# A spectral layer and a gated convolution: three `a1` buffers, another opening, another order on VectorE

## Chip, cores, metric

One Trainium2 chip, the program on one of its cores. The metric is the device time of that core in microseconds; the time of a run is its whole device time, and the span of a profile runs from the core's first to its last instruction.

## What is computed

For 8 sequences of 3136 rows and 256 columns:

```python
X = rfft(x, axis=1)                         # 1569 frequencies
Yr = Xr @ w_r - Xi @ w_i + b_r
Yi = Xr @ w_i + Xi @ w_r + b_i
Y  = soft-threshold(Yr, 0.01), soft-threshold(Yi, 0.01)
y  = irfft(Y, n=3136, axis=1)
h  = relu(y @ w_in)                         # 256 -> 1024
c  = 3-tap convolution of h along the rows, per column
out = (h * sigmoid(c)) @ w_out              # 1024 -> 256
```

`moe_w_in`, `moe_conv_w` and `moe_w_out` arrive as 64-bit floats, so the kernel makes 32-bit values out of their bits itself ("conversion" below).

## The kernel before

The Fourier transform of length 3136 = 49 x 64 is done as two stages of matrix products with a scratch array in HBM between them, and the inverse transform likewise.

*First phase (lines 122 to 479).* Stage 1 (`stage1`) multiplies a tile of `x` (`xr`, 98 partitions, 4 columns `j`, 256) with the matrix `f1`, in two halves of one matmul each; ScalarE copies each half from PSUM to a tile `a1`, and after the second half a DMA stores `a1` to the scratch array `sc1[b]` (392 KB). A batch has 8 such tiles, 16 halves. For batch 0 all of it is done ahead of the loop by `stage1_head`, which has tiles of its own (`ha`) for all eight, and copies by ScalarE and VectorE in turn. For the other batches 112 halves are spread over the loop; `halves()` yields one at a time, and asks for the next tile of `x` when one is used up (three buffers). The list `due` in the loop says how many halves must have been given by the end of each step: 2, 5, 9, 13, 16 for steps 0 to 4, then 3 a step, from step 11 on 2.6 a step on average, until 112 are given in step 40.

The loop has steps `it` of 0 to 52. Three stages of work on 50 items (`batch`, group of four residues) stand one step apart:

- `stage2(it)`: for t in 0, 1 eight transforms with the table `t2` (loaded in slices of four groups), from the tile `a2` that was read back from `sc1`. ScalarE copies the imaginary part to `d` and casts both parts to `fh`; VectorE makes `d` the difference (L306) and `fl` the remainder of `fh` (L307), since products are made from two rounded parts. Then ScalarE casts `d` into `fh` (L309), and VectorE makes "`fl` from `d`" (L311). There is one `d`.
- `mix(it - 1)`: 36 matmuls with the weights, in three PSUM tiles `ps_mx` of one buffer each, in the order c = 2, 0, 1. After c = 2 VectorE adds the bias (L333, `p1`), after c = 0 and 1 it makes `v` (L337, twice each).
- `threshold(it - 2)`: ScalarE's `r` (L346), VectorE's L347 on `v`, ScalarE's cast `sh` (L349), GpSimd's `sl` (L350), which has one buffer.
- `stage3(it - 3)`: 12 matmuls from `sh` and `sl`, ScalarE's copy `z1`, a store to `sc2`.

The order on TensorE, and in the loop also that on VectorE and ScalarE, is the order in which the Python code issues instructions (`manual_schedule`). So the generators are advanced by hand: `some(two, 1)` runs `stage2` to its next `yield`, `some(mx, 8)` issues the next eight matmuls of the mix, `one(k)` a half of stage 1 if the step still has more than `k` to give, `back(n)` up to `n` turns of the conversion. The other queues, SyncE's with the DMAs among them, and all engines ahead of the loop are ordered by a planner with its own costs; `issue_after(ins)` puts what a block issues on `ins`'s queue behind `ins`.

The conversion (`later`) has three turns a step. A turn ends at each `yield`; a `yield "act"` closes the step for it, and at the step's end one more turn issues an operation on ScalarE. It starts in step `WP0` = 7, and the turns run out in step 47.

*Second phase (lines 482 to 603).* For each batch `stage4` reads `sc2` and makes the two parts `yh`, `yl` of the spectral output; `up` multiplies with `w_in`, ScalarE and VectorE do the convolution and the gate, `down` multiplies with `w_out`. The first `up` needs all eight pieces of `stage4` of batch 0.

The body of a loop step before, which the change reorders:

```python
some(two, 1)
th = threshold(...)
ss[it - 2] = next(th, None)      # r and L347
back(2)
some(two, 1)
some(mx, 8); one(1)
some(th, 1)                      # sh and sl
some(two, 1); some(mx, 5)        # L309; p1
...
back(1)
some(two, 1)                     # L311
```

Of the kernel before, what the change touches and what calls it, by code (L numbers as in the profile page):

```python
# [9 lines left out]
F32 = mybir.dt.float32  # L10
# [8 lines left out]
B, S, D, FF = 8, 3136, 256, 1024  # L19
# [9 lines left out]
JC = 4  # L29
# [72 lines left out]
def spectral_ffn_kernel(ctx: ExitStack, tc: tile.TileContext, x, w_r, w_i, b_r, b_i,  # L102
                        w_in, conv_w, w_out, fwd1, fwd2, inv1, inv2, out):
    nc = tc.nc
    K1, K2, KQ, KI = 2 * R, 2 * SP, 2 * R2, 4 * (U + 1)
# [16 lines left out]
    with ExitStack() as ab:  # L122
        stg = ab.enter_context(tc.tile_pool(name="stg", bufs=1))
        wbp = ab.enter_context(tc.tile_pool(name="wbp", bufs=2))
        s1p = ab.enter_context(tc.tile_pool(name="s1p", bufs=2))
# [18 lines left out]
        def split(dst_hi, dst_lo, src):  # L144
            nc.scalar.copy(dst_hi, src)
            nc.vector.tensor_tensor(dst_lo, src, dst_hi.bitcast(F32), op=ALU.subtract)
# [4 lines left out]
        def load_t2(g):  # L151
            sl = slice(g * UG, min((g + 1) * UG, U + 1))
            return nc.sync.dma_start(t2[:, sl, :], fwd2v[:, sl, :])

        def load_mix():

            raw = [stg.tile([P, NT, D], F32, name=f"wm_raw{k}", tag="raw", bufs=2) for k in range(2)]
            for k in range(2):
                ld = nc.sync.dma_start(raw[k], (w_r, w_i)[k].rearrange("(t p) e -> p t e", p=P))
            split(wmix_hi[:, :, 0, :], wmix_lo[:, :, 0, :], raw[1])  # L160
            for k, op in ((1, ALU.subtract), (2, ALU.add)):
                w = stg.tile([P, NT, D], F32, name="wm", tag="wm")
                nc.vector.tensor_tensor(w, raw[0], raw[1], op=op)
                split(wmix_hi[:, :, k, :], wmix_lo[:, :, k, :], w)
            return ld
# [85 lines left out]

        def stage1(b, jc, xr):

            a1 = s1p.tile([K1, JC, D], F32, name="a1", bufs=2)
            for j in range(0, JC, 2):
                ps = ps1.tile([K1, 2, D], F32, name="ps_s1")
                nc.tensor.matmul(ps, f1, xr[:, j:j + 2, :], start=True, stop=True)  # L257
                nc.scalar.copy(a1[:, j:j + 2, :], ps)
                if j + 2 == JC:
                    nc.sync.dma_start(sc1[b][:, jc * JC:(jc + 1) * JC, :], a1)  # L260
                yield None

        def stage1_head(xs, b=0):

            with tc.tile_pool(name="ha", bufs=1, reuse_waits="tile") as ha:
                for jc, xr in enumerate(xs):
                    a1 = ha.tile([K1, JC, D], F32, name=f"ha{jc}")
                    for j in range(0, JC, 2):
                        k = (jc * 2 + j // 2) % 4
                        if k < 3:  # L270
                            ps = psm.tile([K1, 2, D], F32, name="ps_s1h", tag=f"ps_mx{k}")
                        else:
                            ps = ps1.tile([K1, 2, D], F32, name="ps_s1")
                        nc.tensor.matmul(ps, f1, xr[:, j:j + 2, :], start=True, stop=True)  # L274
                        if j:
                            nc.vector.tensor_copy(a1[:, j:j + 2, :], ps)
                        else:
                            nc.scalar.copy(a1[:, j:j + 2, :], ps)
                    st = nc.sync.dma_start(sc1[b][:, jc * JC:(jc + 1) * JC, :], a1)
            return st  # L280

        def load_a2(b, g):
            a2 = a2p.tile([KQ, UG, D], F32, name="a2")
            if g < NG:
                rows = slice(g * 4 * UG, (g + 1) * 4 * UG)
                ld = nc.sync.dma_start(a2, sc1[b][rows].rearrange("(u q) j d -> (q j) u d", q=4))
            else:
                for k in range(UG):
                    ld = nc.sync.dma_start(a2[0:R2, k, :], sc1[b + k][4 * U:K1].rearrange("q j d -> (q j) d"))
            return a2, ld  # L290
# [51 lines left out]
        def threshold(v):  # L342
            sh = wk.tile([K2, UG, D], F32R, name="sh")
            sl = wk.tile([K2, UG, D], F32R, name="sl", bufs=1)
            r = wk.tile([K2, UG, D], F32, name="r", bufs=1)
            nc.scalar.activation(r, v, AF.Relu, bias=mlam)  # L346
            nc.vector.scalar_tensor_tensor(v, v, LAM, r, op0=ALU.add, op1=ALU.min)  # L347
            yield sh, sl
            nc.scalar.copy(sh, v)  # L349
            SL_ENG.tensor_tensor(sl, v, sh.bitcast(F32), op=ALU.subtract)  # L350
            yield None
# [17 lines left out]
        def some(g, n):  # L369
            for _ in range(n):  # L370
                next(g, None)
# [5 lines left out]
        items = [(b, g) for b in range(B) for g in range(NG)]  # L377
        for b in (0, UG):
            items.insert(items.index((b + UG - 1, 0)), (b, NG))
        n_it = len(items)  # L380
        firsts = [(b, jc) for b in range(B) for jc in range(NQ)]
        WP0 = NG + 1
        a2s = {}
        load_f1()
        with tc.tile_pool(name="hx", bufs=1, reuse_waits="tile") as hx:
            xh = []
            for p in range(NQ):
                xr, ld = load_x(hx, 0, p, parts=2 if p == 0 else 1, tag=f"hx{p}")
                xh.append(xr)
            with tc.issue_after(ld.ins):  # L390
                st = stage1_head(xh)
        asked = []

        def ask():
            asked.append(load_x(s1p, *firsts[NQ + len(asked)], bufs=XRB)[0])

        def halves():
            for n in range(NQ, len(firsts)):
                yield from stage1(*firsts[n], asked[n - NQ])
                while len(asked) < n - NQ + XRB and len(asked) < len(firsts) - NQ:  # L400
                    ask()

        first = halves()
        with tc.issue_after(st.ins):
            ld = load_mix()
        with tc.issue_after(ld.ins):
            ld = load_t2(0)
        ab.enter_context(tc.manual_schedule(engines={mybir.EngineType.PE}))
        with tc.issue_after(ld.ins):
            ask()  # L410
            some(first, 2)
            a2s[0], ld = load_a2(*items[0])
        with tc.issue_after(ld.ins):
            load_bias()
            a2s[1], ld = load_a2(*items[1])
            for _ in range(2):
                ask()
        ab.enter_context(tc.issue_after(ld.ins))
        wkf, wk, cab, io = [ab.enter_context(tc.tile_pool(name=nm, bufs=n, reuse_waits="tile"))
                            for nm, n in (("wkf", 2), ("wk", 2), ("cab", 1), ("io", 2))]  # L420
# [3 lines left out]
        i1_hi = cab.tile([K2, U + 2, KQ], F32R, name="i1_hi")  # L424
        i1_lo = cab.tile([K2, U + 2, KQ], F32R, name="i1_lo")
        background = later()
        given, held = 2, []
        xs, vs, ss, i1s = {}, {}, {}, {}
        ab.enter_context(tc.manual_schedule(engines={mybir.EngineType.DVE, mybir.EngineType.Activation}))
        for it in range(n_it + 3):  # L430
            xs[it], vs[it - 1] = [], []
            two = stage2(items[it][1], a2s.pop(it), xs[it]) if it < n_it else iter(())
            mx = mix(xs.pop(it - 1), vs[it - 1]) if 0 <= it - 1 < n_it else iter(())
            due = (2, 5, 9, 13, 16)[it] if it < 5 else 16 + 3 * (it - 4) if it <= 10 else 34 + 13 * (it - 10) // 5
            n_a, given = due - given, due
            work = 3 if WP0 <= it < n_it else 0

            def one(k=0):
                some(first, n_a > k)

            def back(n):
                for _ in range(n if work else 0):
                    if not held:
                        held[:] = [0] * (next(background, None) == "act")

            if it <= NG:
                with tc.issue_after(ld.ins) if it + 2 < NG else ExitStack():
                    if it + 3 <= NG:
                        load_t2(it + 1)
                    if it + 3 == NG:  # L450
                        load_t2(NG - 1)
                        load_t2(NG)
                    i1s[it] = load_inv1(it)
            some(two, 1)
            th = threshold(vs.pop(it - 2)[0]) if 0 <= it - 2 < n_it else iter(())
            ss[it - 2] = next(th, None)
            back(2)
            some(two, 1)
            some(mx, 8)
            one(1)  # L460
            some(th, 1)
            some(two, 1)
            some(mx, 5)
            if it - 1 in i1s:
                split(*i1s.pop(it - 1))
            back(1)
            some(two, 1)
            some(mx, 5 if n_a > 3 else 9)
            one(2)
            some(mx, 9)  # L470
            one(3)
            some(mx, 64)
            if held:
                held[:] = [0] * (next(background, None) == "act")
            if 0 <= it - 3 < n_it:
                stage3(*items[it - 3], ss.pop(it - 3))
            one(0)
            if it + 2 < n_it:
                a2s[it + 2], ld = load_a2(*items[it + 2])
# [148 lines left out]
```

## Time and profile before

| | |
|---|---|
| median of 3 runs (lowest, highest) | 1773.59 us (1771.73, 1774.48) |
| profiled execution | 1775.9 us |
| its span | 1774.1 us |
| mean granted TensorE clock | 0.987 |
| busy: TensorE, its weight loads, VectorE, ScalarE, GpSimd | 1730.7, 1608.3, 1487.7, 1209.1, 118.5 us |
| HBM read, written | 86.02 MB, 77.59 MB |

PE is TensorE's matmuls, PEld its weight loads, DVE VectorE, ACT ScalarE, POOL GpSimd, SP SyncE, on whose queue all DMAs are issued. "L311" is line 311 of the kernel. A row of a timeline has start, duration, engine, line, operation, output<-inputs, shape, count, and in brackets the idle time of the engine before it and who ended it. Neighbouring instructions of one line are merged (x4). One 32-bit matmul counts as two in the rows.

### The profile page before, as it was taken

What the parts mean: (1) busy time and instruction counts of PE and PEld (TensorE: products, weight loads), DVE (VectorE), ACT (ScalarE), POOL (GpSimd) and SP (SyncE); (2) the same over time, 40 slices, a digit from 0 to 9 for tenths busy, and PEclk for the clock granted to TensorE, in tenths of its full rate; (3) what the DMA queues carried; (4) which work ended last, traced back from release to release, by engine and by line L of the source; (5) the groups of instructions that cost most, each with busy time, mean ns of one, the idle gap of its engine ahead of it and who ended that gap; (6) DMA issues with size and microseconds to landing.
All of it is one profiled execution on the core that took longest, in us unless ns stands there. A gap on an engine that the chain in (4) does not pass through costs nothing.

```text
span 1774.1 us, 28820 instructions
## 1 busy us (share of the span) xinstructions
PE 1730.7 (98%) x11872; PEld 1608.3 (91%) x11872; DVE 1487.7 (84%) x1757; ACT 1209.1 (68%) x1565; POOL 118.5 (7%) x54
## 2 busy tenths in 40 slices
PE   6999999999888999999999999999999999999999
PEld 2788888888888999999999999999999999999998
DVE  2778898898994988888888888888888888888887
ACT  2567677677554777777777777777777777777766
POOL 0122222222221000000000000000000000000000
PEclk8999999999988999999999999999999999999999
DMA  8777677666424110111111111111101111100001
GB/s 249 223 236 243 213 230 251 219 224 217 127 93 129 38 40 22 38 46 46 50 48 47 46 40 49 50 40 50 49 21 40 49 50 40 49 22 21 22 21 42
DMA packets 108304, 165.47 MB, mean 93 GB/s; under 512 B 8492, under 2 KB 86316, under 8 KB 108174
## 3 DMA queue, kind: packets, MB, share of 16 engines
q1 hardware_dynamic: 108174, 163.64, 29.1%
q8 instruction: 94, 1.54, 0.3%
q14 instruction: 36, 0.29, 0.0%
HBM read 86.02 MB, written 77.59 MB: 92 GB/s over the span
## 4 chain that ended last, share of the span: by engine, by line
PE 92%; DVE 3%; DMA 3%; issue 1%; ACT 1%; SPq 0%; POOL 0%; ACTq 0%
PE acc L557 31%; PE ps_h L529 31%; PE ps_mx L329 9%; PE ps_s L510 7%; PE ps_s L257 5%; PE ps_s L301 4%; PE ps_s L360 3%; DVE v L337 1%; DMA sc<-a 1%; DMA t<-in_fwd_dram 1%; PE ps_s1h L274 1%; ACT r L346 1%; DMA xr<-in_x_dram 0%; DMA z<-sc 0%; DVE p L333 0%
## 5 line engine op out<-in xcount | busy, mean ns | idle before, releaser
L557 PE MATMUL acc<-wout,gh 128*128 128x256 f32 x3136 | 567.4, 280 | 0.0
L529 PE MATMUL ps_h<-yh,win 128*128 128x450 f32 x1792 | 550.1, 368 | 0.0
L538 DVE SCALAR_TENSOR_TENSOR c<-h,cw,c 128x896 f32<-128x896 f32 x448 | 513.5, 1148 | 38.9 <-ACT c L536 37.3
L557 PEld LDWEIGHTS acc<-wout,gh 128*128 128x128 f32 x3136 | 490.1, 188 | 5.1
L557 PE MATMUL acc<-wout,gl 128*128 128x256 f32 x1568 | 437.4, 280 | 0.0
L531 ACT ACTIVATE h<-ps_h 128x900 f32<-128x900 f32 x224 | 207.4, 926 | 260.4 <-PE ps_h L529 260.4
L529 PEld LDWEIGHTS ps_h<-yh,win 128*128 128x128 f32 x1792 | 339.0, 189 | 26.1 <-DVE yl L517 0.4
L529 PE MATMUL ps_h<-yl,win 128*128 128x450 f32 x896 | 329.4, 368 | 0.0
L544 DVE TENSOR_TENSOR gl<-c,gh 128x896 fp32r<-128x896 f32 x224 | 243.2, 1089 | 76.1 <-ACT gh L543 74.6
L557 PEld LDWEIGHTS acc<-wout,gl 128*128 128x128 f32 x1568 | 293.8, 188 | 0.6
L540 DVE TENSOR_TENSOR c<-h,c 128x896 f32<-128x896 f32 x224 | 243.4, 1087 | 48.1 <-ACT c L539 48.1
L543 ACT CAST gh<-c 128x896 fp32r<-128x896 f32 x224 | 211.1, 943 | 70.3 <-DVE c L540 68.3
L539 ACT ACTIVATE c<-c 128x896 f32<-128x896 f32 x224 | 213.0, 951 | 8.3 <-DVE c L538 4.5
L329 PE MATMUL ps_mx<-wmix_hi,fl 128*128 128x256 f32 x600 | 188.0, 313 | 7.6 <-DVE fl L311 7.6
L329 PE MATMUL ps_mx<-wmix_hi,fh 128*128 128x256 f32 x600 | 185.5, 309 | 1.8 <-DVE p L333 1.5
L529 PEld LDWEIGHTS ps_h<-yl,win 128*128 128x128 f32 x896 | 169.3, 189 | 10.9
L536 ACT ACTIVATE c<-h,cw 128x896 f32<-128x896 f32 x168 | 176.1, 1048 | 2.2 <-DVE gl L544 0.2
L329 PE MATMUL ps_mx<-wmix_lo,fh 128*128 128x256 f32 x600 | 171.1, 285 | 0.0
L350 POOL TENSOR_TENSOR sl<-v,sh 128x1024 fp32r<-128x1024 f32 x50 | 118.3, 2366 | 423.3 <-PE ps_s L360 321.6
L337 DVE TENSOR_TENSOR v<-ps_mx,p 64x512 f32<-64x512 f32 x200 | 137.5, 687 | 7.7 <-PE ps_mx L329 4.8
L329 PEld LDWEIGHTS ps_mx<-wmix_hi,fl 128*128 128x128 f32 x600 | 115.5, 192 | 21.1 <-issue 12.0
L510 PEld LDWEIGHTS ps_s<-i,z 100*128 100x128 f32 x1024 | 130.4, 202 | 4.6 <-DVE yl L517 2.2
(84 smaller groups left out, 1963.6 us busy)
## 6 DMA issues: line engine op xcount, KB each, us to landing
z<-sc SPq DMA_DIRECT2D x64, 400.0 KB
xr<-in_x_dram SPq DMA_DIRECT2D x63, 392.0 KB
a<-sc SPq DMA_DIRECT2D x48, 512.0 KB
sc<-z SPq DMA_DIRECT2D x48, 512.0 KB
out_dram<-o SPq DMA_DIRECT2D x27, 896.0 KB
sc<-a SPq DMA_DIRECT2D x56, 392.0 KB
sc<-ha SPq DMA_DIRECT2D x8, 392.0 KB
win_bits<-in_moe_w_in_dram SPq DMA_DIRECT2D x4, 512.0 KB
```

Source lines behind the costliest of these rows:

```text
L329: nc.tensor.matmul(ps[c][:, k, :], lt, rh, start=(n == 0), stop=(n == len(mm) - 1))
L337: nc.vector.tensor_tensor(v[dst, :, k, :], ps[c][src], p1[src, c], op=ALU.add)
L510: nc.tensor.matmul(ps[:, t, j * K1:(j + 1) * K1], z2[:, j, t * P:(t + 1) * P], i2, start=(j == 0), stop=(j == JG - 1), skip_group_check=True)
L529: nc.tensor.matmul(ps[:, a, 0:CH + 2], lt, rh, start=(n == 0), stop=(n == len(mm) - 1))
L531: nc.scalar.activation(h, ps[:, :, 0:CH + 2], AF.Relu)
L536: nc.scalar.mul(c, h[:, :, 0:CH], cw[:, 0, f:f + 1])
L538: nc.vector.scalar_tensor_tensor(c, h[:, :, k:k + CH], cw[:, k, f:f + 1], c, op0=ALU.mult, op1=ALU.add)
L539: nc.scalar.activation(c, c, AF.Sigmoid)
L540: nc.vector.tensor_tensor(c, h[:, :, 1:CH + 1], c, op=ALU.mult)
L543: nc.scalar.copy(gh, c)
L544: nc.vector.tensor_tensor(gl, c, gh.bitcast(F32), op=ALU.subtract)
L557: nc.tensor.matmul(acc[m // 2][:, m % 2, :], lt[:, sl], rh[:, f, :], start=(f == 0 and n == 0 and m % 2 == 0), stop=(f == NF - 1 and n == ...
```

## The change

- The tile `a1` of stage 1 gets three buffers instead of two.
- The opening. The weights' load and split (`load_mix`) and the first slice of `t2` are issued right behind the loads of `x` for batch 0, ahead of `stage1_head` in the code, instead of behind its last store. Behind that store now comes `a2` of step 0 at once, then the first tile of `x` for the loop, the bias, `a2` of step 1, two more tiles of `x`. The first two halves of stage 1, which were issued ahead of step 0, are given in step 0 (`given` starts at 0), where they come behind its transforms. TensorE's order by hand begins a little later in the code.
- In a loop step both `t` of `stage2` come first. `threshold` is cut in three: `r`; L347; `sh` and `sl`. L347 stands behind `p1`, L311 right behind L347, and `sh` and `sl` behind the mix's c = 0 matmuls have begun. On VectorE: both pairs of L306 and L307, a turn of the conversion, L333, a turn, L347, L311, a turn, L337.
- The conversion starts in step 5, again with three turns a step, one at each of three places.

```diff
-            a1 = s1p.tile([K1, JC, D], F32, name="a1", bufs=2)
+            a1 = s1p.tile([K1, JC, D], F32, name="a1", bufs=3)
...
             nc.scalar.activation(r, v, AF.Relu, bias=mlam)
+            yield sh, sl
             nc.vector.scalar_tensor_tensor(v, v, LAM, r, op0=ALU.add, op1=ALU.min)
-            yield sh, sl
+            yield None
             nc.scalar.copy(sh, v)
...
             with tc.issue_after(ld.ins):
+                load_mix()
+                load_t2(0)
                 st = stage1_head(xh)
...
         with tc.issue_after(st.ins):
-            ld = load_mix()
-        with tc.issue_after(ld.ins):
-            ld = load_t2(0)
-        ab.enter_context(tc.manual_schedule(engines={mybir.EngineType.PE}))
+            a2s[0], ld = load_a2(*items[0])
         with tc.issue_after(ld.ins):
             ask()
-            some(first, 2)
-            a2s[0], ld = load_a2(*items[0])
-        with tc.issue_after(ld.ins):
             load_bias()
             a2s[1], ld = load_a2(*items[1])
             for _ in range(2):
                 ask()
+        ab.enter_context(tc.manual_schedule(engines={mybir.EngineType.PE}))
...
-        given, held = 2, []
+        given, held = 0, []
...
-            work = 3 if WP0 <= it < n_it else 0
+            work = 5 <= it < n_it
...
-            some(two, 1)
+            some(two, 2)
             th = threshold(vs.pop(it - 2)[0]) if 0 <= it - 2 < n_it else iter(())
+            some(mx, 8)
+            back(1)
             ss[it - 2] = next(th, None)
-            back(2)
-            some(two, 1)
-            some(mx, 8)
             one(1)
-            some(th, 1)
             some(two, 1)
             some(mx, 5)
             if it - 1 in i1s:
                 split(*i1s.pop(it - 1))
             back(1)
+            some(th, 1)
             some(two, 1)
+            back(1)
             some(mx, 5 if n_a > 3 else 9)
             one(2)
+            some(th, 1)
             some(mx, 9)
             one(3)
             some(mx, 64)
```

## Prediction

> **What bounds the kernel now.** I read the table of stretches first, cut where the chain of waits changes its character: opening loads, filling, steady first phase, last steps of the first phase, hand-over, second phase. Columns: stretch, length, busy time of PE, PEld, DVE, ACT, POOL with instruction counts, granted clock, DMA share, GB/s.
>
> ```profile
> 0.00:24.00 24.00, 18.69 (x32) 6.42 (x32) 5.59 (x10) 6.17 (x10) 0.20 (x4) 1.00 0.78 242
> 24.00:44.00 20.00, 7.82 (x26) 4.99 (x27) 5.84 (x11) 5.37 (x10) 0.00 (x0) 0.66 0.98 256
> 44.00:101.00 57.00, 51.80 (x327) 41.27 (x325) 41.99 (x65) 34.07 (x58) 8.95 (x4) 0.94 0.70 213
> 101.00:442.00 341.00, 340.55 (x2433) 293.05 (x2434) 301.12 (x493) 242.50 (x391) 82.25 (x36) 1.00 0.72 231
> 442.00:529.00 87.00, 75.72 (x585) 71.75 (x584) 83.64 (x126) 49.23 (x76) 22.39 (x10) 0.96 0.37 117
> 529.00:569.00 40.00, 35.32 (x221) 34.45 (x221) 15.86 (x22) 16.10 (x17) 4.70 (x2) 0.76 0.41 133
> 569.00:1774.00 1205.00, 1200.83 (x8256) 1156.33 (x8255) 1033.63 (x1033) 855.69 (x1005) 0.00 (x0) 1.00 0.13 40
> ```
>
> TensorE is never idle for long in 101 to 442 and in 569 to 1774: 1546 of 1774 us can change only if TensorE's own work does, and the diff leaves every matmul in place. What is open is 0 to 101, bound by loads (DMA 0.98 busy in 24 to 44), and 442 to 569, where VectorE is busy 83.64 of 87 us and then the hand-over to the second phase follows.
>
> The chain of waits through the opening (start, length, what):
>
> ```profile
> 24.10 4.86 DMA sc<-ha
> 32.37 10.85 DMA t<-in_fwd_dram
> ...
> 53.69 8.00 DMA sc<-a
> 62.41 2.02 PE ps_s L257 x2
> 64.44 2.35 PE ps_mx L329 x11
> 66.78 1.71 PE ps_s L257 x2
> ...
> 90.85 6.51 DMA sc<-a
> 97.38 3.94 DMA a<-sc
> ```
>
> Three places: the head's last store lands at 28.96 and only then may step 0's `a2` be asked for; step 1 starts at 43.22, when the second slice of `t2` has landed; at 53.69 ScalarE waits 8 us for the store of an `a1` of which there are two.
>
> How long a step is in the steady part, from the chain's last piece of step 40, a half of stage 1, which ends at 441.38 where step 41 begins:
>
> ```profile
> 440.52 0.86 PE ps_s L257 x2
> ```
>
> Step 6 starts when the load asked for at 97.38 has landed, at 101.4. 35 steps to 441.38 are 9.71 us each. The due list gives 112 - 19 = 93 halves to them, 2.66 a step at 0.86, 2.29 us. So TensorE needs 9.71 - 2.29 = 7.4 us for a step without halves, and from step 41 on there are none.
>
> VectorE's rows of step 41, the first of these, in order:
>
> ```profile
> 443.21 0.42 DVE L306 TENSOR_TENSOR d<-ps_s,d 128x256 f32<-128x256 f32 x1 [1.92 <-ACT fh L305]
> 443.55 0.68 DVE L307 TENSOR_TENSOR fl<-ps_s,fh 128x512 fp32r<-128x512 f32 x1
> 444.26 1.23 DVE L347 SCALAR_TENSOR_TENSOR v<-v,r 128x1024 f32<-128x1024 f32 x1
> 445.40 0.69 DVE L196 SCALAR_TENSOR_TENSOR wout_e<-wout_bits,wout_e 128x512 int32<-128x512 int32 x1
> 446.00 0.42 DVE L197 TENSOR_SCALAR wout_m<-wout_bits 128x512 int32<-128x512 int32 x1
> 446.34 0.42 DVE L306 TENSOR_TENSOR d<-ps_s,d 128x256 f32<-128x256 f32 x1
> 446.67 0.68 DVE L307 TENSOR_TENSOR fl<-ps_s,fh 128x512 fp32r<-128x512 f32 x1
> 447.27 1.29 DVE L333 TENSOR_TENSOR p<-ps_mx,bias 128x512 f32<-128x512 f32 x2
> 448.46 0.69 DVE L311 TENSOR_TENSOR fl<-d,fh 128x512 fp32r<-128x512 f32 x1
> 449.06 2.81 DVE L337 TENSOR_TENSOR v<-ps_mx,p 64x512 f32<-64x512 f32 x4
> ```
>
> From 443.21 to 451.87 is 8.66 us; the two conversion operations take 446.34 - 445.40 = 0.94 of it. 7.7 us is thus VectorE's own step, a little over TensorE's 7.4. The later steps are longer for a reason that three rows show: the group of L311 over 441 to 530 (count, busy, mean ns), step 44's L311, and GpSimd's row beside it.
>
> ```profile
> L311 DVE TENSOR_TENSOR fl<-d,fh 128x512 fp32r<-128x512 f32 x9 | 12.9, 1433 | 0.0
> ```
> ```profile
> 476.38 1.80 DVE L311 TENSOR_TENSOR fl<-d,fh 128x512 fp32r<-128x512 f32 x1
> ```
> ```profile
> 475.27 2.36 POOL L350 TENSOR_TENSOR sl<-v,sh 128x1024 fp32r<-128x1024 f32 x1 [7.33 <-ACT sh L349]
> ```
>
> L311 takes 0.69 in step 41 and 1.80 in step 44, where it starts inside GpSimd's `sl` (475.27 to 477.63) and ends 0.55 after it. VectorE's other rows of step 41 read PSUM for one input; L311 reads `d` and `fh`, both in SBUF. The rule in the Trainium skill, SBUF — State Buffer, section Who interferes with whom, is that such an operation and a GpSimd one that reads SBUF exclude each other for a whole instruction, the first to start winning; the trace agrees, 1.80 against 0.69.
>
> The hand-over: VectorE's last work of step 49, then the chain.
>
> ```profile
> 527.02 2.12 DVE L337 TENSOR_TENSOR v<-ps_mx,p 64x512 f32<-64x512 f32 x3
> ```
> ```profile
> 534.96 2.36 POOL sl L350
> 537.37 1.56 PE ps_s L360 x11
> ...
> 544.45 2.04 PE ps_s L510 x16
> 546.51 5.68 DMA z<-sc
> 552.32 16.61 PE ps_s L510 x80
> ```
>
> **The change part by part.**
>
> *Third `a1`.* Removed: the wait from 53.69 to 61.70. Its price on TensorE: the next 2 + 11 + 2 matmuls take 2.02, 2.35 and 1.71 us (62.41 to 68.49), where halves take 0.86 and 11 of the mix some 1.3 (7.4 less 1.8 for the transforms and 1.4 for stage 3, for 36). That is 3.1 us lost to a slow clock behind the pause, and the pause itself is the one row in the list of waits from 50 to 64 that names it:
>
> ```profile
> PE ps_s L257 <- ACT a L258: 3.8, 1, 3.8
> ```
>
> Together 6.9. Next in line are the loads of `x`: DMA is 0.70 busy over this stretch, so they can come earlier, but not for nothing. Bounds: 0 (a load of `x` is as late) and 6.9; I take 6.5, nearer the upper end because of the 0.30 of free DMA.
>
> *Opening loads.* The weights (2 x 256 KB) and the first `t2` slice go ahead of the head's stores, in a stretch with DMA 0.78 busy; at 242 GB/s they are 3.2 us. But step 0's `a2` still waits for the last store, which they push back by about 1 us (the stores queue behind them and catch up in the 0.22 of free time), and now nothing stands between store and `a2`: DMA rests for the 3.94 us of a lone `a2` load (97.38) less its transfer of 512 KB, 2 us. What was moved past the pause is one `x` tile (392 KB by its shape, 1.6 us), which now follows `a2`. Ahead of `t2`'s second slice, for which step 1 waits, stands the same list as before. So step 1 starts between 3 us earlier (no pause) and 4 later; by the bytes I take 1.5 later. The three weight splits (five VectorE operations of the 0.69 kind, three on ScalarE) fall into the head, where VectorE is busy 5.6 of 24 us: nothing, if the queues hold them behind the copies whose data come first; if not, they hold up copies, PSUM and TensorE (a rival).
>
> *Two halves into step 0*: they leave the place ahead of step 0's transforms and stand between these and step 1, in the wait for `t2`: nothing; without that wait 2 x 0.86.
>
> *Steps 2 to 5* are then TensorE's own. Before step 6 stand the store of the 16th half and the load behind it (6.51 + 3.94 us), with the same distance as now, but DMA has to carry the same bytes in some 5 us less: I give back 0.5. **Opening: +1.5 - 6.5 + 0.5 = -4.5 us.**
>
> *Steady steps*: in a step VectorE now does both `d`/`fl` pairs, `p`, then L347 and L311, then the four L337. ScalarE's `r` runs beside the first; `sh` and GpSimd's `sl` come later, but `sl` had to wait for stage 3 at the end of the step anyway. The first L337 moves back by at most 1.9 us (1.23 + 0.69), and what it frees is needed only by the next step's mix. VectorE is busy 301 of 341 us: cost 0, and if that slack is gone up to 1 us a step (a rival).
>
> *Late steps, 41 to 49.* (a) L311 now follows L347 at once, while `sl` has to wait for `sh`, which has to wait for L347: L311 is through before `sl` starts, and the four L337 (2.81 us, one input in PSUM) cover the 2.36 of `sl`. Gone: 9 x (1.43 - 0.69) = 6.7 us. (b) `r` waits for the last L337 of the step before; L347 stood right behind it and now stands behind 3 us of other work. (c) Conversion has three slots a step as before, starting in step 5 instead of 7. Counting the generator's turns, the last lands in step 45, not 47 (nor 40), and of the 14 VectorE operations now in 41 to 47 ten remain. So nine steps at 7.7 and ten operations at some 0.54 (0.69 and 0.42 overlapping by 0.08): 69.3 + 5.4 = 74.7 us from 443.21, against 529.14 - 443.21 = 85.9 now. **-11.2 us.** Bounds: nothing but the four operations and half of L311's loss, -5.5; and TensorE's 7.4 for all nine steps, -13.9.
>
> *Hand-over.* At the end of step 49 the mix of the last item no longer waits for a blocked L311. Stage 3 of item 48 now ends at 538.9, 9.8 us behind VectorE's 529.14. With the pieces in a row it is the last mix part and stage 3 (1.4 + 1.4), then `sl` behind `sh` (2.4), then 1.4: some 7.5. The last `sl` and its stage 3 follow with the same spacing or less. **-2 us** (0 to -3). The loads behind the stores (5.68) and the 16.61 us I leave.
>
> Sum: -4.5 - 11.2 - 2 = -17.7. The profiled execution took 1775.9 us (span 1774.1 and 1.8 around it), which gives 1758.2; the median of the runs, 1773.6, is 2.3 lower, so 1755.9.
>
> **Rivals.**
>
> *The opening gives nothing (22%).* Either `x` is as late as `a1` was, or weight splits stand in VectorE's queue ahead of copies whose data are there. For it: DMA 0.98 busy right behind the head. Against: 0.70 where the wait is. -13.2 or, with the head held up by 4 us, -9: 1760 to 1764.5.
>
> *The hand-over stays at full clock (13%).* The 16.61 us are 80 matmuls at half clock:
>
> ```profile
> 555.00:560.00 5.00, 5.00 (x26) 5.00 (x25) 1.26 (x2) 2.00 (x2) 0.00 (x0) 0.50 0.34 90
> ```
>
> At the 2.04 us for 16 just before, they would take 10.2, so -6.4 more: 1749.5. It needs a shorter pause ahead of them. The Trainium skill, TensorE: Matmul & The Clock Gate, Part 1, would have the clock return after some 3.4 us of sustained work; the trace does not agree, busy 5.00 of 5.00 at 0.50 for over 16 us. By the rule the stretch would cost about 5 us less already today, and the change would move nothing there.
>
> *Late steps do not fall to 7.7 (10%).* ScalarE or the order on TensorE then sets some 8.6 (what step 41 took): -3 instead of -11.2, 1764.
>
> *No change, or slower (7%).* L337 behind L347 and L311 makes the mix of the next step wait for PSUM in the steady part. At 17.7/35 = 0.5 us a step it cancels the rest (3% for that), beyond it decides (4%); at 1 us a step +35 - 17.7: 1791. Against: VectorE's 40 us of slack there, and the step in which those results are not wanted.
>
> **How the numbers follow.** My case has 48%, 1752 to 1759 by itself. The range is 1747 to 1766: it holds the first three rivals' times and leaves out the last rival, a head held up for longer, and two rivals at once. A measurement of this kernel cannot tell 0.2% (3.5 us) from no change: faster 0.93, the first four cases; same 0.03 and slower 0.04, the last rival's two halves.
>
> **What would show it.** No 8 us wait for an `a1` store in the chain; step 6's transforms near 97; L311 at 0.69 in the late group; last conversion operation in step 45; step 49's last L337 near 513; the 80 matmuls at 16 to 17 us. Wrong if the late group keeps 1.4, if the head ends after 26, or if TensorE shows idle time between 101 and 440.

## The result and the profile after

The changed kernel takes 1758.15 us (median; 1753.32 to 1759.99) against 1773.59 (1771.73 to 1775.54) for the kernel before: ratio 0.9908, 95% interval 0.989 to 0.9926. The forecast was 1755.9, with a range of 1747 to 1766. The sum came out; two of its three terms did not. In the changed kernel L347 to L350 are L348 to L351, stage 3's L360 is L361, `stage4`'s L510 is L509, `up`'s L529 is L528.

The profiled execution of the changed kernel is its slowest, 1759.99 (span 1758.2). The table of stretches, cut at the same places and with the same columns:

```profile
0.00:24.00 24.00, 17.95 (x29) 6.05 (x30) 6.04 (x12) 5.94 (x10) 0.20 (x4) 1.00 0.82 235
24.00:44.00 20.00, 7.51 (x24) 4.33 (x22) 5.22 (x9) 5.00 (x10) 0.00 (x0) 0.72 0.74 209
44.00:101.00 57.00, 51.72 (x339) 42.62 (x340) 40.31 (x66) 34.34 (x59) 9.43 (x4) 0.95 0.78 241
101.00:442.00 341.00, 341.00 (x2425) 293.46 (x2425) 298.16 (x495) 242.05 (x391) 81.61 (x35) 0.99 0.72 229
442.00:529.00 87.00, 81.04 (x671) 78.42 (x671) 81.54 (x133) 55.69 (x83) 26.86 (x12) 1.00 0.39 128
529.00:569.00 40.00, 37.44 (x222) 35.48 (x221) 19.57 (x24) 19.81 (x22) 0.58 (x1) 0.83 0.45 130
```

TensorE is never idle from 101 to 442. The DMA share falls from 0.98 to 0.74 in 24 to 44, where the loads set the pace, and rises by only 0.04 in 0 to 24. In busy time over 0 to 44 that is 24 x 0.82 + 20 x 0.74 = 34.5 us, against 38.3 before: 3.8 us less carried. The chain of waits through the opening shows where these are missed:

```profile
26.63 4.83 DMA sc<-ha
...
35.74 11.19 DMA t<-in_fwd_dram
46.93 0.14 issue
47.06 3.37 PE ps_s L301 x16
...
88.82 7.12 DMA sc<-a
95.95 3.90 DMA a<-sc
99.85 0.14 issue
99.98 2.75 PE ps_s L301 x16
102.74 1.71 PE ps_mx L329 x8
```

Step 1 starts at 47.06, 3.7 us later than before (43.35). The 8 us wait for an `a1` store is gone, and step 6 starts at 99.98 (before 101.45). But the matmuls behind that pause take longer (2.75 and 1.71 us, at a granted clock of 0.62 over both; before 2.02 and 0.94, at 1.00), and step 41 starts at 441.36, before 441.22. In the profiles the opening gave nothing.

The late steps did: VectorE's rows at both ends, the last operation of the conversion, GpSimd's `sl` beside the L337 of step 49, and the group of L311 over 441 to 530.

```profile
443.35 0.42 DVE L306 TENSOR_TENSOR d<-ps_s,d 128x256 f32<-128x256 f32 x1 [1.17 <-ACT fh L305]
```
```profile
481.57 0.68 DVE L210 TENSOR_TENSOR wout<-wout_m,wout_rest 128x512 fp32r<-128x512 f32 x1
```
```profile
514.48 2.81 DVE L337 TENSOR_TENSOR v<-ps_mx,p 64x512 f32<-64x512 f32 x4
515.22 2.41 POOL L351 TENSOR_TENSOR sl<-v,sh 128x1024 fp32r<-128x1024 f32 x1 [5.26 <-ACT sh L350]
```
```profile
L311 DVE TENSOR_TENSOR fl<-d,fh 128x512 fp32r<-128x512 f32 x9 | 6.1, 680 | 0.0
```

From 443.35 to 517.29 are 73.94 us, where 85.93 were; L311 takes 0.68 us instead of 1.43, and is over before `sl` starts; the L337 beside `sl` keep their 0.7 us each. The conversion ends in step 45, at 482.25. The hand-over follows, in the chain:

```profile
521.91 0.39 PE ps_s L361
522.30 3.35 PE ps_s L509 x31
525.65 4.71 DMA z<-sc
530.50 2.00 PE ps_s L509 x16
...
535.73 6.04 DMA z<-sc
541.77 0.14 issue
541.90 10.53 PE ps_s L509 x48
552.43 6.19 PE ps_h L528 x24
```

From the last L337 of step 49 to the first `up` (552.14) are 34.85 us, before 39.50. The second phase takes 1206.06 against 1205.46. So by stretches: opening +0.1, late steps -12.0, hand-over -4.7, second phase +0.6; together -16, which is the difference of the spans (15.9).

### The profile page after: what moved, and what is told of

It reads as the page before. It is cut to its first block, busy times and chain, and to the rows that moved or that the text cites. A ratio compares the mean times of both kernels' runs of the same rounds, so it can differ in the third digit from the quotient of the medians.

```text
span 1758.2 us, 28865 instructions
## 1 busy us (share of the span) xinstructions
PE 1721.6 (98%) x11872; PEld 1602.2 (91%) x11872; DVE 1472.0 (84%) x1757; ACT 1206.8 (69%) x1565; POOL 118.7 (7%) x54
## 4 chain that ended last, share of the span: by engine, by line
PE 93%; DMA 2%; DVE 2%; issue 1%; ACT 0%; SPq 0%; DVEq 0%; ACTq 0%
PE ps_h L528 31%; PE acc L556 31%; PE ps_mx L329 11%; PE ps_s L509 6%; PE ps_s L257 5%; PE ps_s L301 5%; PE ps_s L361 3%; DMA t<-in_fwd_dram 1%; DMA z<-sc 1%; DVE v L337 0%; DMA sc<-a 0%; DVE p L333 0%; DMA sc<-ha 0%; DVE fl L307 0%; DVE v L348 0%
## 5 line engine op out<-in xcount | busy, mean ns | idle before, releaser
L528 PE MATMUL ps_h<-yh,win 128*128 128x450 f32 x1792 | 550.6, 368 | 0.0
L528 PEld LDWEIGHTS ps_h<-yh,win 128*128 128x128 f32 x1792 | 339.4, 189 | 26.1 <-DVE yl L516 0.4
L528 PE MATMUL ps_h<-yl,win 128*128 128x450 f32 x896 | 329.7, 368 | 0.0
L528 PEld LDWEIGHTS ps_h<-yl,win 128*128 128x128 f32 x896 | 169.4, 189 | 11.0
L351 POOL TENSOR_TENSOR sl<-v,sh 128x1024 fp32r<-128x1024 f32 x50 | 118.5, 2370 | 410.7 <-PE ps_s L361 254.1
L337 DVE TENSOR_TENSOR v<-ps_mx,p 64x512 f32<-64x512 f32 x200 | 137.4, 687 | 2.9
L301 PEld LDWEIGHTS ps_s<-t,a 128*128 128x128 f32 (+1 forms) x800 | 99.7, 198 | 39.6 <-issue 28.8
L509 PEld LDWEIGHTS ps_s<-i,z 100*128 100x128 f32 x1024 | 128.1, 198 | 5.8 <-issue 3.0
```

Of the source, the lines that this page charges most:

```text
L301: nc.tensor.matmul(ps[:, k], a2[0:rows, k, t * P:(t + 1) * P], t2[0:rows, u, :], start=(k == 0), stop=(k == UG - 1), skip_group_check=True)
L509: nc.tensor.matmul(ps[:, t, j * K1:(j + 1) * K1], z2[:, j, t * P:(t + 1) * P], i2, start=(j == 0), stop=(j == JG - 1), skip_group_check=True)
L528: nc.tensor.matmul(ps[:, a, 0:CH + 2], lt, rh, start=(n == 0), stop=(n == len(mm) - 1))
```

## Experiments

Marks used below are those of the prediction: start of a step's transforms, "late" from VectorE's first `d` of step 41 to the last L337 of step 49, "hand-over" from there to the first `up`. The kernels were run in three groups of four. Each group has a chip of its own, on which the kernel before was run too (its medians: 1775.5, 1775.0, 1776.4); a ratio is always to the kernel before in the same group.

### Parts of the change

**Old opening**, with three `a1`, the new loop, conversion from step 5.

```diff
-                load_mix()
-                load_t2(0)
                 st = stage1_head(xh)
...
-            a2s[0], ld = load_a2(*items[0])
+            ld = load_mix()
+        with tc.issue_after(ld.ins):
+            ld = load_t2(0)
         with tc.issue_after(ld.ins):
             ask()
+            some(first, 2)
+            a2s[0], ld = load_a2(*items[0])
```

> The changed kernel with the opening of before (weights, first t2 slice and the first two halves back in their old places); three a1 buffers and the new order of the steps stay. In the changed kernel the head's last store is issued at 26.63 instead of 24.10, step 1 starts at 47.06 instead of 43.35 and step 6 at 99.98 instead of 101.45. Theory A, the new opening costs: the weight splits hold up the head and DMA rests behind its last store. Then step 1 starts near 43.4, step 3 near 62, step 6 at 94 to 96, and the time is 4 to 6 us below the changed kernel's. Rival B, DMA has so many bytes to carry before step 6 that the order doesn't matter: step 1 near 43.4, but step 6 at 99 to 101 and the time within 1.5 us of the changed kernel's.

1754.14 us, ratio 0.988 (0.9866 to 0.9894): below the changed kernel, which ran on another chip; the last group has both on one. Step 6 starts at 93.75, step 41 at 433.54, late 73.96.

**Two `a1`**, everything else as changed (`bufs=3` back to 2).

> The changed kernel with two a1 buffers. Theory A: the third buffer took away the 8 us wait for a store, worth 6.4 us between the transforms of steps 2 and 3 (9.83 us in the changed kernel, 16.3 before). With two the wait is back, steps 2 to 3 take 15 to 16 us, and since step 6 then starts some 5 us later the time is 4 to 6 us above the changed kernel's. Rival B: what the third buffer gives is given back before step 6, where the store of the 16th half and the load behind it are late anyway; step 6 starts within 1.5 us of 99.98 and the time is the same.

1758.04, ratio 0.9902 (0.9889 to 0.9914): the time of the changed kernel. The marks fit neither theory: steps 2 to 3 take 11.0 us (theory A 15 to 16), and step 6 starts at 102.89 (rival B within 1.5 of 99.98), in a profile whose last head store is issued only at 29.54. From step 1 to step 6 it takes 55.3 us, the changed kernel 52.9 and, in its second profile, 52.4. So under the new opening the third buffer is worth nothing that the times show, and 2 to 3 us by these profiles. TensorE's wait for an `a1` is still there, but shorter:

```profile
PE ps_s L257 <- ACT a L258: 2.0, 2, 1.3
```

It was 3.8 us before, with a slow clock behind it, and is 1.3 at the longest here. That steps 1 and 2 are late themselves, and leave less to wait for, is the likely reason.

**The loop's new order alone**: opening, `a1` and conversion as before (three turns a step from step 7).

> Before, with nothing but the new order inside a loop step (threshold cut in three, L347 behind p1, L311 right behind L347); two a1 buffers, old opening, conversion from step 7. Theory A: the late steps lose the 6.7 us of blocked L311 and the wait for r. From d of step 41 to the last L337 of step 49 VectorE takes 69.3 us for nine steps and 14 conversion operations at 0.54, 77 us, against 85.9 before; with 3 to 4 us at the hand-over the time is 11 to 13 us below before. Rival B: the steps were bound by the order on ScalarE or TensorE, and only conversion moved out of them helped: 82 us or more, and less than 5 us below before.

1761.53, ratio 0.9921 (0.9909 to 0.9933), late 76.10, L311 at 0.68. That is 14.0 us below the kernel before on this chip, where the whole change gained 15.4 in its own runs: nearly all of it comes from the order in the loop. Late is 9.8 us shorter than before, with the same 14 operations of the conversion in it: 6.8 are L311, 1.3 VectorE's waits for `r` ahead of L347, which are gone, and 0.7 two operations of the conversion that were longer beside `sl` (L198 1.21 us against 0.68, L191 0.54 against 0.42). About 1 us is spread over other rows. The hand-over gives another 3.5 (36.00). Beside the old opening (1754.14, same chip) it lacks the third `a1` and two steps of conversion: 7.4 us. Late shows 2.1 of them (76.10 against 73.96), which leaves about 5 for the third `a1` in the old opening. The profiles have step 6 at 101.06 without it and 93.75 with it; 2.0 of these 7.3 us are there at step 1 already, ahead of any wait for an `a1`, so that 5.3 lie between steps 1 and 6. No run adds the third buffer alone.

**Conversion from step 5 alone**, in the kernel before.

```diff
-            work = 3 if WP0 <= it < n_it else 0
+            work = 3 if 5 <= it < n_it else 0
```

> Before, with the conversion from step 5 instead of 7 and nothing else. Theory A: four VectorE operations leave steps 41 to 47, some 2.2 us of the 85.9, or up to 3.5 if one of them was itself blocked by GpSimd's sl; the time is 2 to 3.5 us below before. Rival B: in these steps VectorE's waits (for r, for sl) fill what the conversion leaves, and the stretch stays at 85 to 86 us.

1775.3, ratio 0.9996 (0.9985 to 1.0008): nothing. Four operations left the late steps, but late is 87.03 us (before 85.93). L311 is blocked for 1.1 us more in all, and in step 41 an operation of the conversion, L191, is shut out in its place:

```profile
L311 DVE TENSOR_TENSOR fl<-d,fh 128x512 fp32r<-128x512 f32 x9 | 14.0, 1558 | 0.0
```
```profile
447.69 2.36 POOL L350 TENSOR_TENSOR sl<-v,sh 128x1024 fp32r<-128x1024 f32 x1 [5.89 <-PE ps_s L360]
447.71 2.62 DVE L191 TENSOR_SCALAR wout_e<-wout_bits 128x512 int32<-128x512 int32 x1
```

L191 took 0.54 us in the kernel before; it and L311 together cost 3.2 us more, and the four operations would be worth some 2.2 at the prediction's 0.54 each. So an operation of the conversion pays as L311 does where it stands in `sl`'s time, and taking work from VectorE ahead of that only brings it to the wait earlier. The same four operations are worth 2.1 us once L311 is out of the way.

### Is it the overlap with GpSimd?

**L311 in the middle of the L337**: the changed kernel, with L311 behind the first two L337.

```diff
             some(th, 1)
-            some(two, 1)
             back(1)
             some(mx, 5 if n_a > 3 else 9)
             one(2)
             some(th, 1)
             some(mx, 9)
+            some(two, 1)
             one(3)
```

> The changed kernel, but L311 (VectorE's fl from d) is moved behind the first two L337 of its step, so that it falls into the time of GpSimd's sl again. Theory A: L311 and sl exclude each other for a whole instruction, so L311's mean in the late steps rises from 0.68 to about 2 us (it starts inside sl and ends about 0.5 us behind it), the stretch from d of step 41 to the last L337 of step 49 grows from 73.9 by about 9 x 1.4 = 12 us to 84 to 88, and the time to 1768 to 1772. Rival B: what the new order gained is that the transforms of the next step, L347 and the first PSUM results are no longer in the way of each other, not the overlap with GpSimd; then L311 stays at about 0.7, the stretch at 74 to 76, and the time at 1758 to 1760.

1802.72, ratio 1.0146 (1.012 to 1.0171): slower than the kernel before, and 30 us above theory A's time. GpSimd's `sl` and VectorE's rows around it, then L311's groups over 441 to 530 and 101 to 442 (this kernel reaches step 41 only at 460.42; over its steps 41 to 49 the mean of L311 is 2.26 us):

```profile
481.72 2.36 POOL L351 TENSOR_TENSOR sl<-v,sh 128x1024 fp32r<-128x1024 f32 x1 [7.88 <-PE ps_s L361]
```
```profile
480.37 1.38 DVE L337 TENSOR_TENSOR v<-ps_mx,p 64x512 f32<-64x512 f32 x2
481.78 2.85 DVE L311 TENSOR_TENSOR fl<-d,fh 128x512 fp32r<-128x512 f32 x1
484.66 1.39 DVE L337 TENSOR_TENSOR v<-ps_mx,p 64x512 f32<-64x512 f32 x2
```
```profile
L311 DVE TENSOR_TENSOR fl<-d,fh 128x512 fp32r<-128x512 f32 x9 | 22.5, 2500 | 0.3
```
```profile
L311 DVE TENSOR_TENSOR fl<-d,fh 128x512 fp32r<-128x512 f32 x33 | 61.7, 1871 | 1.0
```

L311 starts 0.06 us behind `sl` and ends 0.55 behind its end. That is theory A's blocking, larger than expected: late is 90.23 us, 16.3 more than in the changed kernel, of which L311's own time is 9 x (2.26 - 0.68) = 14.2. The steady steps take 22 us more (step 6 at 98.81, step 41 at 460.42, 361.6 us where 339.8 are usual), where no expectation had any. VectorE is then busy 339 of 359 us there, and TensorE waits for L311:

```profile
PE ps_mx L329 <- DVE fl L311: 14.6, 18, 1.7
```

The Trainium skill, SBUF — State Buffer, section Who interferes with whom, has the same exclusion, the first to start winning; here `sl` was first by 0.06 us, and L311 paid for all of it. This kernel also has L311 two L337 later in the step; how much of the 22 us is that place, and not the blocking, is not shown.

**Conversion out of the late steps**: old opening, new loop, and a second turn in the first slot of each even step, so that the last operation falls into step 41.

```diff
-            back(1)
+            back(2 - it % 2)
```

> The opening of before, everything else as changed (three a1, the new order in the loop), and conversion with a second turn in the first slot of every even step, so that its last operation falls into step 41 instead of 45. Theory A (the prediction's sum of the late steps): nine steps at VectorE's own 7.7 us and what conversion is left in them, at 0.54 us an operation; without the ten operations the stretch from d of step 41 to the last L337 of step 49 falls from 74 to about 69 us, and the time to about 1750 (old opening with the changed loop took 1754.1). Rival B: TensorE's 7.4 us a step or ScalarE sets the end as soon as VectorE has slack, so that the stretch stays above 72 and the time above 1752. Rival C: the additional turns in the steady steps take VectorE's slack there, and step 41 starts more than 1 us later than the 433.5 of the old opening with the changed loop.

1750.34, ratio 0.985 (0.9826 to 0.9874), the fastest of all kernels here. Late is 69.89 us, with two operations of the conversion left in it:

```profile
436.91 0.42 DVE L306 TENSOR_TENSOR d<-ps_s,d 128x256 f32<-128x256 f32 x1 [1.77 <-ACT fh L305]
...
440.57 0.68 DVE L210 TENSOR_TENSOR wout<-wout_m,wout_rest 128x512 fp32r<-128x512 f32 x1
```
```profile
504.00 2.80 DVE L337 TENSOR_TENSOR v<-ps_mx,p 64x512 f32<-64x512 f32 x4
```

These two take 0.6 each of VectorE's time; the nine steps thus take 7.63 us each, and the eight operations that left were worth (73.96 - 69.89) / 8 = 0.51 each. Rival B falls. So does C, though step 41 started 1.4 us later (434.92) than in the old opening's profile: so did step 6 (95.12 against 93.75), and the steady steps took the added turns for nothing (step 6 to 41: 339.80 us, old opening 339.79).

### The opening

**The kernel before once more**, for a second profile.

> The kernel of before once more, for a second profile. The hand-over from the last L337 of step 49 to the first up took 39.50 us in its first profile, and 33.7 to 36.0 us in four kernels that leave the code of the hand-over alone, among them one in which only the conversion was moved. Theory A: the hand-over varies by several us between executions of one kernel, and this run gives 34 to 37 us. Rival B: 39.5 us belongs to this kernel, and comes again within 1 us. The other marks should come again within 1 us: step 1 at 43.4, step 6 at 101.5, the late stretch 85.9.

Step 1 at 43.69, step 6 at 98.49, step 41 at 438.29, late 85.97, hand-over 39.24. Late and hand-over repeat within 0.3 us; the opening differs by 3 us between two executions of one kernel, more than expected. So one profile settles no opening to less than that, and the medians decide.

**Weight splits behind the head's copies**; the loads stay early.

```diff
                 st, c_act, c_dve = stage1_head(xh)
+            with tc.issue_after(c_act.ins), tc.issue_after(c_dve.ins):
+                split_mix(raw)
```

> The changed kernel, but with the splits of the three weights given to the queues of ScalarE and VectorE only behind the head's last copies; the loads of the weights and of the first t2 slice stay ahead of the head's stores. Theory A: what the new opening costs is that copies of the head stand behind weight splits which wait for their loads (ScalarE 3.15 us, VectorE 2.26 us in the changed kernel), so that the last store is issued at 26.63 instead of 24.10. Then the last store is issued near 24, step 1 starts near 44.5, step 6 near 97, and the time is 2 to 3 us below the changed kernel, 1755 to 1756. Theory B: the cost lies behind the last store, where the first a2 now waits alone while the weights' transfers no longer fill that gap, and in the order of the loads after it. Then the store is issued earlier, but step 1 still starts at 46 or later, step 6 at 99 or later, and the time is within 1 us of the changed kernel, 1757 to 1759.

1757.99, ratio 0.9891 (0.9872 to 0.9911), no faster than the changed kernel. In the changed kernel ScalarE's and VectorE's queues do stand behind the load of a weight, with copies of the head behind:

```profile
20.70 0.62 ACT L145 CAST wmix_hi<-wm_raw 128x512 fp32r<-128x512 f32 x1 [3.15 <-DMA wm_raw<-in_w_i_dram]
21.23 0.58 ACT L278 COPY ha<-ps_s1h 98x512 f32<-98x512 f32 x1
```
```profile
20.78 0.69 DVE L163 TENSOR_TENSOR wm<-wm_raw,wm_raw 128x512 f32<-128x512 f32 x1 [2.26 <-DMA wm_raw<-in_w_i_dram]
```

With the splits behind, the last store is issued at 21.17, but it takes 7.62 us where the changed kernel's took 4.83; it lands at 28.79, no earlier than in the kernel before (28.96):

```profile
21.17 7.62 DMA sc<-ha
```

That the store queues behind the transfers of the weights is the likely reason. The step marks are theory A's (step 1 at 43.71, step 6 at 97.43), and the time is theory B's: in this profile step 41 starts at 437.23, 1.7 us ahead of the changed kernel's second profile below, and the hand-over is 1.6 longer (36.10 against 34.50). So what the splits' place is worth stays open by 2 us.

The last group put the changed kernel and the old opening on one chip again, with two more openings.

> The changed kernel once more, beside the old opening and two other openings on one chip. Theory A: the opening is what the change lost, as the earlier runs had it (old opening with the rest changed 1754.1, changed kernel 1758.2); then this kernel is 3 to 5 us slower than the old opening here too, its last head store is issued at 26 or later, step 1 starts at 46 or later and step 6 at 99 or later. Theory B: the differences between openings are those between executions (the kernel of before had step 6 at 101.45 in one profile and at 98.49 in another); then the medians of these four kernels lie within 2 us of each other.

1758.48, ratio 0.9894 (0.9873 to 0.9916); last head store issued at 26.90, step 1 at 46.79, step 6 at 99.16, step 41 at 438.97.

> The opening of before with everything else as changed, for the second time. Theory A: 3 to 5 us below the changed kernel of the same call, last head store at 23 to 25, step 1 at 42 to 44.5, step 6 at 93.5 to 95.5. Theory B: within 2 us of the changed kernel, with the marks of its opening as far from those of its first profile as the profiles of before are from each other, 3 us.

1753.04, ratio 0.9862 (0.9837 to 0.9887); 23.26, 41.84, 92.98, 432.79. Theory A: the new opening costs 5.4 us on this chip, where no run of the one kernel reaches the other's (1749.18 to 1755.92, and 1756.09 to 1759.12). The old opening's marks come again within 1 us of its first profile. Step 1's transforms and the matmuls behind them, in the changed kernel and with the old opening:

```profile
46.79 3.75 PE ps_s L301 x16
50.54 1.62 PE ps_mx L329 x8
52.16 0.86 PE ps_s L257 x2
```
```profile
41.84 2.02 PE ps_s L301 x16
43.86 0.95 PE ps_mx L329 x8
44.81 0.86 PE ps_s L257 x2
```

3.75 + 1.62 against 2.02 + 0.95: steps 0 and 1 start 10.5 us apart (36.29, 46.79) in the one and 4.3 (37.50, 41.84) in the other. The granted clock over step 1's transforms is 0.50 and 1.00, and TensorE needs 2.4 us more for the same work. The length of the pause does not settle the clock alone. The kernel with the conversion out of the late steps, whose opening is the old one, has a pause of 1.65 us here, and a granted clock of 0.50 all the same:

```profile
40.92 3.76 PE L301 MATMUL ps_s<-t,a 128*128 128x128 f32 x16 [1.65 <-DMA t<-in_fwd_dram]
```

The old opening's first profile has a pause of 1.77 us there and 2.02 for the transforms.

**Weights behind the first `a2`**, the first `t2` slice early.

```diff
-                load_mix()
                 load_t2(0)
                 st = stage1_head(xh)
...
             a2s[0], ld = load_a2(*items[0])
+        with tc.issue_after(ld.ins):
+            ld = load_mix()
```

> The changed kernel, but the weights are loaded behind the first a2 and so split there; the first t2 slice stays ahead of the head's stores. Theory A: the hold-up of the head by the weights' loads and splits is the cost. Then the last head store is issued near 23.5, step 1 (before which the same bytes must land) starts near 43.5, and the time is at or below that of the old opening, some 4 us below the changed kernel. Theory B: what costs is that the first a2 is asked for first behind the stores and waits there alone, with DMA at rest; then step 1 starts at 45 or later, and the time is within 1.5 us of the changed kernel.

1759.54, ratio 0.9894 (0.9869 to 0.9918): theory B. The head is not held up (last store at 24.45), and yet step 1 starts at 47.38. The stretch 24 to 32 by itself, for this kernel, the changed kernel (its second profile), and the old opening:

```profile
24.00:32.00 8.00, 0.00 (x0) 0.00 (x0) 0.38 (x1) 0.00 (x0) 0.00 (x0) 0.79 0.55 185
```
```profile
24.00:32.00 8.00, 2.02 (x5) 0.34 (x3) 2.75 (x5) 1.59 (x3) 0.00 (x0) 0.75 0.62 206
```
```profile
24.00:32.00 8.00, 0.00 (x0) 0.00 (x0) 2.57 (x4) 1.24 (x2) 0.00 (x0) 0.61 0.98 266
```

DMA is busy 0.55 and 0.62 of these 8 us where the first `a2` is next behind the last store, 0.98 where weights, `t2` and a tile of `x` stand between: 3.6 and 3.0 us of rest. No run fills this gap and leaves the rest of the new opening alone.

**First two halves ahead of step 0 again**, in the kernel with the splits behind.

> The kernel with the splits behind the head's copies (1758.0 in its first run), but with the first two halves of stage 1 ahead of step 0 again, as before the change. Theory A: TensorE work in steps 0 and 1 stands beside the wait for t2, so the place of the two halves is worth nothing; the time is 1757 to 1759 and step 6 starts as in the kernel with the splits behind, at 97.4 within 1.5 us. Theory C: the two halves in steps 0 and 1 delay these steps, or the store of their a1 comes too late for the a2 of step 2; then step 2 starts 2 us earlier than the 11.1 us behind step 1 that it took there, and the time is 1754 to 1756, that of the old opening.

1755.87, ratio 0.9879 (0.9857 to 0.9901): in theory C's range, 2.1 us below the kernel with the splits behind in the other group; step 2 starts 8.7 us behind step 1 (there 11.1), step 6 at 95.06. Step 0 starts later here (39.09), step 1 only 5.1 behind it, and its transforms keep their clock:

```profile
44.23 2.02 PE ps_s L303 x16
```

Between the two groups that difference is within the intervals, and step 1 was slow in the profile of the additional turns too, where the two halves also stand ahead of step 0. So the place of the halves is a likely part of the cost, not a settled one.

## Why the prediction was right, and where it was not

*Late steps, -11.2: measured -12.0.* Each part was there, and this is the largest term. L311 fell by 9 x 0.75 = 6.8 us (6.7 predicted); the conversion ended in step 45 with ten operations in the stretch; VectorE's own step is 7.63 (7.7), an operation 0.51 (0.54). The remaining part, the wait for `r` that the prediction named without a price, was 1.3. The experiment that put L311 back into `sl`'s time shows that the overlap was the cause; the loop's order alone gives 14.0 us. What the sum didn't say is that the conversion's share depends on L311: 2.1 us with it out of the way, nothing without (1775.3). The sentence that VectorE's other rows of step 41 read PSUM for one input is wrong: L347 and the conversion's operations read and write SBUF alone, and L191 (2.62 us) and L198 (1.21) were shut out as well where they stood in `sl`'s time.

*Opening, -4.5: measured about zero* (+0.1 between the first profiles, +0.7 between the second ones). The third `a1` was sized roughly right for the opening of before: about 5 us by the medians and by the profiles from step 1 to step 6, 6.5 predicted. The step that failed is the opening loads at +1.5: step 1 starts 3.7 us later in the first profiles and 3.1 in the second ones, and the new opening costs 5.4 us on the chip that had both (1758.48 against 1753.04). Three of its statements were wrong. It has the stores "queue behind them and catch up in the 0.22 of free time": the DMA share in 0 to 24 rose by 0.04, 1 us, and not by the 3.2 us of the loads. The pause behind the last store was put at 2 us; the stretches show 3.0 to 3.6. And the place of the two halves was put at nothing, "in the wait for `t2`": putting them back gave 2.1 us, within the intervals, so that this part is likely and not shown. The rest behind the store is read from the DMA shares; it was not tried by itself. Two of the signs failed with it: the head ends after 26 (its last store is issued at 26.6), and step 6, expected near 97, started at 99.98 and 99.16.

So the rival "the opening gives nothing" (22%) is what the opening did. How far by that rival's own cause is open: splits do stand ahead of copies, yet with the splits behind the copies the time is the same (1757.99), though step 6 is 1.7 us earlier in that profile. The rival's times (1760 to 1764.5) were missed because the other two terms gave more.

The give-back is of the same kind. With 3 to 4 us lost ahead of step 1, the third `a1` has less of a wait to take away: two `a1` measure 1758.04, and the longest wait is 1.3 us instead of 3.8. The two terms were added as if each stood alone.

*Hand-over, -2: measured -4.7*, 39.2 to 39.5 in both profiles of before, 34.9 and 34.5 in those of the changed kernel; the other kernels with the new loop, the one with L311 in `sl`'s time aside, spread over 33.3 to 36.9. From the first `stage4` matmul to the first `up` nothing changed (538.77 to 568.63, 522.13 to 552.14). Its start moved from 9.6 us behind the last L337 to 4.8. The mix part in between is the largest piece; its 34 matmuls, before and after:

```profile
526.40:533.60 7.20, 7.04 (x34) 6.84 (x34) 0.56 0.08 31
```
```profile
514.50:519.10 4.60, 4.47 (x34) 4.12 (x34) 1.00 0.30 118
```

2.6 us are clock (0.56 against 1.00). Before, TensorE had waited 1.5 us for the blocked L311 just ahead; that this wait is the cause is not shown, since behind the same wait the second profile of before has 5.90 us for these matmuls, and the changed kernel waits 1.2 us at this place and keeps its clock. The prediction put this mix at full clock. The four pieces that it puts in a row (1.4, 1.4, 2.4 and 1.4) also add up to 6.6 us, not to the 7.5 that it took. Another 1.6 is order: in the changed kernel the first `stage4` matmuls stand ahead of the last eleven of a stage 3, not behind (537.37 to 538.93 in the chain of before). That this order is a matter of the planner, and not of the new loop, is suggested by the kernel with only the conversion moved, which has it too and a hand-over of 35.02; it was not tried by itself. The 48 matmuls behind the last wait still run at a granted clock of 0.50 (10.53 us), so the rival of full clock did not come.

*Steady steps, 0*: 341.00 of 341 us busy, as predicted. The kernel with L311 in `sl`'s time shows how near that rival was: 1.2 us more of VectorE a step, about as much as its 40 us of slack, cost 22 us.

So -4.5, -11.2, -2 became 0, -12, -4.7. The mechanism of the largest term held; that the whole came out is in part luck, since the errors of the first and the last term cancel.

## What to carry to other kernels

An operation that another engine shuts out costs its whole wait, and its cure is a place in the order where a neighbour that isn't shut out covers the other engine; here, work removed ahead of it gave nothing until then. Where transfers set the pace, count the busy time of DMA up to the mark that waits for them. A load moved out of the gap behind a store whose landing the next load needs is not free, even if it fits elsewhere: the openings here that left that gap empty were 2.8 to 6.5 us slower than the old one on one chip. Gains of two edits in one stretch don't add up: size each with the other in place.

## What the runs showed that was not expected

- L311, 0.68 us alone, takes 2.85 where `sl` (2.36 us) starts 0.06 us ahead; 1.2 us more in each steady step cost 22 us in a stretch where VectorE had 40 us of slack in 341. An operation of the conversion of 0.54 us took 2.62 in the same place.
- The opening of one and the same kernel differs by 3 us between executions (step 6 at 101.45 and 98.49), while its steps 6 to 41 (339.8) and its late steps (85.93 and 85.97) come again within 0.1.
- Step 1's transforms take 2.02 us at a granted clock of 1.00 and 3.75 at 0.50. With 9.4 us and more between the starts of steps 0 and 1 they took 3.4 to 3.75 in all six profiles; with 4.3 to 5.3 us between them they took 2.02 in four and 3.76 in one.
